# Where ScalarE casts V, and when the last two of a chunk's four result tiles are stored, in a local/global attention with a gated feed-forward layer

## The chip, the cores and the metric

The kernel runs on one core of a Trainium2 chip. A core has TensorE for matrix products (PE in the profile, its weight loads PEld), VectorE (DVE), ScalarE (ACT), GpSimd (POOL), and SyncE (SP), which here issues every DMA. Each of them works through its own list of instructions in order, and an instruction that has to wait holds up all that stand behind it in its list. The metric is device time in microseconds (us).

## The reference

There are 8 batches of 8 heads, 512 local positions and 32 global ones per head, and a head dimension of 64. A local query sees the local keys within 32 positions and all global keys; a global query sees everything. The result, 4,608 tokens of 512 values, goes through a gated layer with 1,536 hidden units. All is float32.

```
s_ll = where(|i - j| <= 32, scale * q_l @ k_l.T, -1e9)
a_l  = softmax(concat([scale * q_l @ k_g.T, s_ll]))
out_l = a_l @ concat([v_g, v_l])
out_g = softmax(scale * q_g @ k_all.T) @ v_all
x = concat([out_g, out_l])            # heads side by side: 4608 x 512
y = (sigmoid(x @ w_gate) * (x @ w_val)) @ w_out
```

## The kernel before

The tokens are cut into chunks: two halves of batch 0 (256 tokens each, interleaved), then batches 1 to 7 (512 tokens each), and at the end the 256 global tokens of all batches. While TensorE runs the feed-forward layer of one chunk (`ffn_stream`), the attention of the next is mixed into it head by head (`att_events`): a generator yields after every few products, and a queue of events with due times puts the attention's steps in between.

**The feed-forward layer.** A chunk is twelve items, one for each 128 hidden units. An item has 12 products for the gate (`bank_g`), 12 for the value (`bank_v`), both at line 389, and 12 that multiply the item before by `w_out` and add into up to four PSUM tiles (`bank_o`, line 424). Values are split into a rounded part and a rest, which is why each product is made three times. Between them ScalarE takes the tangent of the gate (L397), its absolute value (L404) and an exponential (L403), VectorE clips the gate (L402, `mn`) and multiplies (L407, L408), and `hh` is the item's result in two parts (ScalarE L410, VectorE L411).

**The result tiles.** When the last product of a chunk's twelfth item has been issued, the loop at L428 halves each `bank_o` tile into `ob`, the even ones on VectorE (L432) and the odd ones on ScalarE (L430), and SP stores it (L433, 256 KB). `ob` has two buffers, so that the third tile can be written only after the first one's transfer has landed, and the fourth after the second's.

**The attention of a head.** K and Q (`qk_raw`) and V (`v_raw`, one buffer, 256 KB, L193) are loaded. ScalarE rounds V into the left half of `vhl` (L214), and GpSimd subtracts to get the rest into the right half (L215); only then may the next head's V be loaded. `vhl` has five buffers: four heads' V are read together once more by the global queries (`global_group`, L360). Scores come from TensorE into `bank_x` (L238), VectorE adds the mask and takes the minimum (L252), ScalarE takes the exponential (L255), VectorE scales by the sum (L222), TensorE transposes (L270), ScalarE and VectorE split the result into `pt` (L281, L282), and TensorE multiplies it by `vhl` (L300, L301). Global scores go to `bank_x` and `bank_y` (L317, L319).

**Shared PSUM.** `bank_g`, `bank_v`, `bank_x` and `bank_y` share one ring of four PSUM banks, taken in turn. A product that starts a new bank waits until the bank's readers from four turns ago are done; for a bank that held a gate these are L397 and L402.

**The order.** The Python code gives the program, but a list scheduler that estimates durations decides at build time in which order each engine gets its instructions. `tc.issue_after(ins)` ties the instructions traced under it on `ins`'s engine to come behind `ins` in that engine's list; it adds no wait. The code before uses it only for the first weight conversions.

Of the kernel before, what the change touches and what calls it, by code (L numbers as in the profile page):

```python
# [8 lines left out]
F32 = mybir.dt.float32  # L9
F32R = mybir.dt.float32r  # L10
U32 = mybir.dt.uint32
AF = mybir.ActivationFunctionType
ALU = mybir.AluOpType
# [4 lines left out]
P = 128  # L18
D = 64
# [13 lines left out]
DM = 512  # L33
# [26 lines left out]
def kernel(ctx, tc, qk, v, w_gate, w_val, w_out, out_l, out_g):  # L60
    nc = tc.nc
# [10 lines left out]
    ffn = ctx.enter_context(tc.tile_pool(name="ffn", bufs=1))  # L72
# [38 lines left out]

    fill(FILL[0])
    conv_bufs = []
    anchor = [None]

    w_src = []
    for f in range(NF):
# [91 lines left out]
    def split_v(T):  # L209
        if T["native"]:  # L210
            return
        t = T["v_raw"]
        vhl = spl.tile([P, 8, 2 * D], F32R, name="vhl", bufs=GH + 1)
        nc.scalar.copy(vhl[:, :, 0:D], t)  # L214
        nc.gpsimd.tensor_tensor(vhl[:, :, D:2 * D], t, vhl[:, :, 0:D].bitcast(F32), op=ALU.subtract)  # L215
        T["v"] = vhl

# [10 lines left out]
    def local_unit(T, blocks, x32s, h, col0):  # L228
# [12 lines left out]
        if T["first"]:  # L241
            s_sb = ffn.tile([P, 2, WIN], F32, name="s_first", tag="ob", bufs=2)
# [7 lines left out]
        for i, j in enumerate(blocks):  # L250
            w = slice(*span(j))
            anchor[0] = nc.vector.tensor_tensor_reduce(  # L252
                out=s_sb[:, i, w], in0=s_ps[:, i, w], in1=mid[:, w], scale=-0.125, scalar=3.0e38,
                op0=ALU.add, op1=ALU.min, accum_out=nm[:, i:i + 1])
            nc.scalar.activation(s_sb[:, i, w], s_sb[:, i, w], AF.Exp, bias=nm[:, i:i + 1], scale=-1.0,  # L255
                                 accum_out=sm[:, i:i + 1])
        yield
        nc.vector.tensor_scalar_add(r, sm, 1e-9)
        nc.vector.reciprocal(r, r)
# [109 lines left out]
    def x_split(xt, x32, kt, x0, ntok):  # L369
        xs = slice(x0, x0 + ntok)  # L370
        nc.scalar.copy(xt[:, 0, kt, xs], x32[:, 0:ntok])
        nc.gpsimd.tensor_tensor(xt[:, 1, kt, xs], x32[:, 0:ntok], xt[:, 0, kt, xs].bitcast(F32), op=ALU.subtract)  # L372

    def ffn_stream(items):


        prev = None
        wo = None
        for n_it in range(len(items) + 1):
            if n_it < len(items):  # L380
                C, f = items[n_it]
                ntok, x0, xt = C["ntok"], C["x0"], C["xt"]()
                fs = slice(f * P, (f + 1) * P)
                for w, nm in ((wg, "bank_g"), (wv, "bank_v")):
                    acc = ps.tile([P, 512], F32, name=nm, tag="att", bufs=4)[:, 0:ntok]
                    n = 0
                    for a, c in ((0, 0), (1, 0), (0, 1)):
                        for t in range(KT):
                            nc.tensor.matmul(acc, w[a][:, t, fs], xt[:, c, t, x0:x0 + ntok],  # L389
                                             start=n == 0, stop=n == 11)  # L390
                            n += 1
                        if n < 12:
                            yield ntok / 512
                    if nm == "bank_g":
                        th = ffn.tile([P, 512], F32, name="th", bufs=1)[:, 0:ntok]
                        mn = ffn.tile([P, 512], F32, name="mn", bufs=1)[:, 0:ntok]
                        nc.scalar.activation(th, acc, AF.Tanh, scale=0.5)  # L397
                        if n_it < 2 * NF and n_it % 2:
                            nc.scalar.activation(mn, acc, AF.Relu, scale=-1.0)
                            nc.scalar.activation(mn, mn, AF.Exp, scale=-1.0)  # L400
                        else:
                            nc.vector.tensor_scalar(mn, acc, 0.0, None, op0=ALU.min)  # L402
                            nc.scalar.activation(mn, mn, AF.Exp)  # L403
                        nc.scalar.activation(th, th, AF.Abs)  # L404
                    else:

                        nc.vector.tensor_tensor(acc, acc, mn, op=ALU.mult)  # L407
                        nc.vector.scalar_tensor_tensor(acc, th, 1.0, acc, op0=ALU.add, op1=ALU.mult)  # L408
                        hh = ffn.tile([P, 2, 512], F32R, name="hh", bufs=2)
                        nc.scalar.copy(hh[:, 0, 0:ntok], acc)  # L410
                        nc.vector.tensor_tensor(hh[:, 1, 0:ntok], acc, hh[:, 0, 0:ntok].bitcast(F32), op=ALU.subtract)  # L411
                    yield ntok / 512
                if not (wo is not None and items[n_it - 1][1] == f):
                    wo = ffn.tile([P, 2, DM], F32R, name="wo", bufs=2)
                    nc.sync.dma_start(wo.bitcast(F32), wo_dram[f])
            if prev is not None:
# [5 lines left out]
                for i, (a, c) in enumerate(((0, 0), (1, 0), (0, 1))):  # L422
# [2 lines left out]
                                         start=f2 == 0 and i == 0, stop=f2 == NF - 1 and i == 2)  # L425
                    if f2 == NF - 1 and i == 2:
                        for t in range(nt):
                            ob = ffn.tile([P, DM], F32, name="ob", bufs=2)  # L428
                            if t % 2:
                                nc.scalar.mul(ob, o_ps[t], 0.5)  # L430
                            else:
                                nc.vector.tensor_scalar(ob, o_ps[t], 0.5, None, op0=ALU.mult)  # L432
                            nc.sync.dma_start(C2["dst"][t * P:(t + 1) * P, :], ob)  # L433
                    yield nt / 4
            prev = (C, f, hh, wo) if n_it < len(items) else None

# [169 lines left out]
```

## Time and profile before

| | |
|---|---|
| median of three runs | 1263.77 us (1258.55 to 1264.96) |
| the profiled execution | 1260.87 us, span 1259.1 us |
| mean granted TensorE clock | 0.975 of full speed |
| PE busy | 1182.2 us, 94% of the span |
| DVE, ACT, POOL busy | 782.3, 754.8, 414.9 us |
| SP stores of result tiles | 34, 256 KB each, 3.2 us to landing (median) |
| loads of `v_raw` | 52, 256 KB each, 2.7 us to landing (median) |

The last line of work is the feed-forward layer's, on PE, so the question for each other engine is where PE stood still for it. In rows of the profile, the number in brackets is the engine's idle time before the instruction, with what ended it. In the table of stretches the columns are the stretch, its length, the busy time (and instruction count) of PE, PEld, DVE, ACT and POOL, the granted TensorE clock as a share of full speed, the DMA engines' busy share, and GB/s. Rows with an engine name ending in q show the engine's queue of DMA issues or its sequencer.

### The profile page before, as it was taken

The numbers are of one execution on the slowest core, as the hardware profiler recorded it, in microseconds if no ns is written. First come the engines' busy times: TensorE is split into PE (matmuls) and PEld (weight loads), VectorE is DVE, ScalarE is ACT, GpSimd is POOL, SyncE is SP. The second block draws the span as 40 slices with busy tenths as digits, with TensorE's granted clock in tenths as the row PEclk, the third lists the DMA queues.
The fourth block names the chain that finished last, engine by engine and source line by source line (L and its number), as shares of the span: only waits on it lengthen the run. The fifth ranks groups of instructions, "written<-read, shape, count | busy, mean of one in ns | idle before, by whom it ended". The sixth has DMA issues, their size and how long they took to land.

```text
span 1259.1 us, 19319 instructions
## 1 busy us (share of the span) xinstructions
PE 1182.2 (94%) x6652; PEld 986.0 (78%) x6652; DVE 782.3 (62%) x2186; ACT 754.8 (60%) x1719; POOL 414.9 (33%) x408
## 2 busy tenths in 40 slices
PE   8898999999998999989998998989999899999998
PEld 6676779878786888868786887868777787888897
DVE  6789866666664676556664675656665676633343
ACT  5676776666665666646665665656665666532333
POOL 2334344423533344423533334433433334100000
PEclk9799999999999999989999998999999899999999
DMA  8678754333434333333434333343332432121243
GB/s 278 225 241 256 247 159 133 85 128 91 125 92 120 92 84 116 100 113 92 109 94 127 98 84 100 100 125 83 113 99 85 129 92 87 51 84 67 67 135 117
DMA packets 59490, 151.82 MB, mean 121 GB/s; under 512 B 6144, under 2 KB 19456, under 8 KB 59392
## 3 DMA queue, kind: packets, MB, share of 16 engines
q1 hardware_dynamic: 59392, 150.59, 39.6%
q8 instruction: 52, 0.85, 0.3%
q14 instruction: 46, 0.38, 0.1%
HBM read 135.36 MB, written 15.20 MB: 120 GB/s over the span
## 4 chain that ended last, share of the span: by engine, by line
PE 66%; DVE 11%; ACT 8%; DMA 7%; POOL 4%; issue 4%; SPq 0%; POOLq 0%; DVEq 0%; ACTq 0%
PE bank_o L424 18%; PE bank_v L389 17%; PE bank_g L389 16%; DMA v_raw<-in_v_dram 5%; PE bank_x L238 4%; PE bank_y L270 3%; POOL vhl L215 3%; ACT s_sb L255 3%; DMA out_dram<-ob 2%; DVE p_buf L222 2%; PE bank_x L300 2%; PE bank_x L301 2%; PE bank_x L317 1%; DVE xt L144 1%; DVE s_sb L252 1%
## 5 line engine op out<-in xcount | busy, mean ns | idle before, releaser
L389 PE MATMUL bank_v<-xt,wv 128*128 128x512 f32 (+1 forms) x1440 | 332.5, 368 | 9.7 <-DVE pt L282 9.7
L424 PE MATMUL bank_o<-wo,hh 128*128 128x512 f32 x1224 | 337.6, 408 | 3.0 <-DVE hh L411 2.0
L389 PE MATMUL bank_g<-xt,wg 128*128 128x512 f32 (+1 forms) x1440 | 333.8, 367 | 0.9 <-POOL xt L372 0.5
L389 PEld LDWEIGHTS bank_v<-xt,wv 128*128 128x128 f32 x1440 | 240.6, 192 | 46.6 <-issue 9.3
L389 PEld LDWEIGHTS bank_g<-xt,wg 128*128 128x128 f32 x1440 | 239.1, 191 | 38.7 <-issue 2.1
L424 PEld LDWEIGHTS bank_o<-wo,hh 128*128 128x128 f32 x1224 | 222.6, 194 | 44.5 <-DVE hh L411 2.8
L203 POOL TENSOR_TENSOR kl<-qk_raw,qk_hi 128x704 fp32r<-128x704 f32 x52 | 88.7, 1705 | 235.7 <-ACT qk_hi L202 229.2
L255 ACT ACTIVATE s_sb<-s_sb,nm 128x192 f32<-128x192 f32 (+1 forms) x240 | 110.6, 462 | 91.8 <-DVE nm L252 91.5
L305 POOL TENSOR_TENSOR x<-t 64x256 f32<-64x256 f32 x104 | 76.2, 733 | 207.5 <-DVE t L304 187.9
L222 DVE TENSOR_SCALAR p_buf<-s_sb,r 128x128 f32<-128x128 f32 (+2 forms) x443 | 116.7, 301 | 8.0 <-PE bank_y L270 2.4
L402 DVE TENSOR_SCALAR mn<-bank_g 128x512 f32<-128x512 f32 (+1 forms) x108 | 67.5, 625 | 84.1 <-ACT th L397 83.2
L411 DVE TENSOR_TENSOR hh<-bank_v,hh 128x512 fp32r<-128x512 f32 (+1 forms) x120 | 72.9, 608 | 60.7 <-ACT hh L410 60.7
L407 DVE TENSOR_TENSOR bank_v<-bank_v,mn 128x512 f32<-128x512 f32 (+1 forms) x120 | 73.7, 614 | 56.0 <-PE bank_v L389 39.8
L304 DVE TENSOR_TENSOR t<-bank_x,t 64x512 f32<-64x512 f32 x104 | 70.7, 680 | 60.5 <-ACT t L303 59.8
L397 ACT ACTIVATE th<-bank_g 128x512 f32<-128x512 f32 (+1 forms) x120 | 63.8, 531 | 73.3 <-PE bank_g L389 72.9
L410 ACT CAST hh<-bank_v 128x512 fp32r<-128x512 f32 (+1 forms) x120 | 62.6, 522 | 72.3 <-DVE bank_v L408 70.7
L252 DVE CUSTOM_DVE_ANT_0 s_sb<-bank_x,masks 128x192 f32<-128x192 f32 (+1 forms) x240 | 80.6, 369 | 34.4 <-PE bank_x L238 25.8
L215 POOL TENSOR_TENSOR vhl<-v_raw,vhl 128x512 fp32r<-128x512 f32 x52 | 67.3, 1294 | 104.0 <-ACT vhl L214 103.3
L282 DVE TENSOR_TENSOR pt<-bank_y,pt 128x512 fp32r<-128x512 f32 x104 | 71.1, 684 | 33.8 <-ACT pt L281 33.7
L270 PE MATMUL bank_y<-ident,p_buf 128*128 128x128 f32 x496 | 80.4, 282 | 10.5 <-DVE p_buf L222 5.8
L270 PEld LDWEIGHTS bank_y<-ident,p_buf 128*128 128x128 f32 x496 | 62.5, 144 | 28.8 <-DVE p_buf L222 6.7
L214 ACT CAST vhl<-v_raw 128x512 fp32r<-128x512 f32 x52 | 32.1, 618 | 87.1 <-DMA v_raw<-in_v_dram 84.8
(110 smaller groups left out, 1770.1 us busy)
## 6 DMA issues: line engine op xcount, KB each, us to landing
wo<-wo_dram SPq DMA_DIRECT2D x116, 512.0 KB, 3.6
qk_raw<-in_qk_dram SPq DMA_DIRECT2D x104, 312.0 KB, 4.5
v_raw<-in_v_dram SPq DMA_DIRECT2D x52, 256.0 KB, 2.7
out_dram<-ob SPq DMA_DIRECT2D x34, 256.0 KB, 3.2
xt<-in_w_gate_dram SPq DMA_DIRECT2D x12, 512.0 KB, 4.4
xt<-in_w_val_dram SPq DMA_DIRECT2D x12, 512.0 KB, 4.1
xt<-in_w_out_dram SPq DMA_DIRECT2D x12, 512.0 KB, 4.2
v_nat<-in_v_dram SPq DMA_DIRECT2D x8, 512.0 KB, 4.9
```

What stands on the lines that cost most here:

```text
L203: nc.gpsimd.tensor_tensor(kl, t[:, K0:Q1], hi[:, K0:Q1].bitcast(F32), op=ALU.subtract)
L215: nc.gpsimd.tensor_tensor(vhl[:, :, D:2 * D], t, vhl[:, :, 0:D].bitcast(F32), op=ALU.subtract)
L222: nc.vector.tensor_scalar(out, in_, by, None, op0=ALU.mult)
L252: anchor[0] = nc.vector.tensor_tensor_reduce(out=s_sb[:, i, w], in0=s_ps[:, i, w], in1=mid[:, w], scale=-0.125, scalar=3.0e38, op0=ALU.add ...
L255: nc.scalar.activation(s_sb[:, i, w], s_sb[:, i, w], AF.Exp, bias=nm[:, i:i + 1], scale=-1.0, accum_out=sm[:, i:i + 1])
L270: nc.tensor.transpose(pt_ps[:, 2 * i + t], pb[:, i, t * P:(t + 1) * P], ident)
L282: nc.vector.tensor_tensor(pt[:, 1], pt_ps, pt[:, 0].bitcast(F32), op=ALU.subtract)
L305: nc.gpsimd.tensor_tensor(dst, t0[:, :, 0], t0[:, :, 1], op=ALU.add)
L389: nc.tensor.matmul(acc, w[a][:, t, fs], xt[:, c, t, x0:x0 + ntok], start=n == 0, stop=n == 11)
L407: nc.vector.tensor_tensor(acc, acc, mn, op=ALU.mult)
L411: nc.vector.tensor_tensor(hh[:, 1, 0:ntok], acc, hh[:, 0, 0:ntok].bitcast(F32), op=ALU.subtract)
L424: nc.tensor.matmul(o_ps[t], ph[:, a, t * P:(t + 1) * P], pwo[:, c], start=f2 == 0 and i == 0, stop=f2 == NF - 1 and i == 2)
```

## The change

Two things are changed. The cast of V (L214) is tied behind the exponential that was traced last before it. And of a chunk's four result tiles, the last two are no longer stored where the chunk ends: they are kept in a list, and stored in the next item, after the absolute value of its gate's tangent; the odd one, on ScalarE, is tied behind that instruction. Chunks of 256 tokens have two tiles only, so for these and for the last item of all nothing is put off.

```diff
-    anchor = [None]
+    anchor, exp_at = [None], [None]
...
-        nc.scalar.copy(vhl[:, :, 0:D], t)
+        with tc.issue_after(exp_at[0].ins):
+            nc.scalar.copy(vhl[:, :, 0:D], t)
...
-            nc.scalar.activation(s_sb[:, i, w], s_sb[:, i, w], AF.Exp, bias=nm[:, i:i + 1], scale=-1.0,
-                                 accum_out=sm[:, i:i + 1])
+            exp_at[0] = nc.scalar.activation(s_sb[:, i, w], s_sb[:, i, w], AF.Exp, bias=nm[:, i:i + 1], scale=-1.0,
+                                             accum_out=sm[:, i:i + 1])
...
+    def store_out(C, t, after=None):
+        ob = ffn.tile([P, DM], F32, name="ob", bufs=2)
+        if t % 2:
+            with tc.issue_after(after.ins) if after is not None else nullcontext():
+                nc.scalar.mul(ob, C["o"][t], 0.5)
+        else:
+            nc.vector.tensor_scalar(ob, C["o"][t], 0.5, None, op0=ALU.mult)
+        nc.sync.dma_start(C["dst"][t * P:(t + 1) * P, :], ob)
...
-                        nc.scalar.activation(th, th, AF.Abs)
+                        last_th = nc.scalar.activation(th, th, AF.Abs)
+                        while later:
+                            store_out(*later.pop(0), after=last_th)
...
                         for t in range(nt):
-                            ob = ffn.tile([P, DM], F32, name="ob", bufs=2)
-                            if t % 2:
-                                nc.scalar.mul(ob, o_ps[t], 0.5)
+                            if t >= 2 and n_it < len(items):
+                                later.append((C2, t))
                             else:
-                                nc.vector.tensor_scalar(ob, o_ps[t], 0.5, None, op0=ALU.mult)
-                            nc.sync.dma_start(C2["dst"][t * P:(t + 1) * P, :], ob)
+                                store_out(C2, t)
```

The scheduler's lists show what this moves. Line numbers in the changed kernel are higher: L215 is its cast of V, L256 the exponential, L379 and L381 the tiles' halving on ScalarE and VectorE, L382 their store, L408 and L415 the tangent and the absolute value, L413 `mn`, L414 its exponential, L423 the cast of `hh`, L428 the load of `wo`.

ScalarE where a chunk ends (the tiles `bank_o_4633` and `bank_o_4635` are the second and fourth of the chunk whose stores stand at 545 us in the profile), before:

```order
L214 CAST vhl<-v_raw 128x8x64
L410 CAST hh<-bank_v 128x512
L255 ACTIVATE s_sb,sm<-s_sb,nm 128x192
L255 ACTIVATE s_sb,sm<-s_sb,nm 128x224
L214 CAST vhl<-v_raw 128x8x64
L430 ACTIVATE ob<-bank_o_4633 128x512
L255 ACTIVATE s_sb,sm<-s_sb,nm 128x224
L255 ACTIVATE s_sb,sm<-s_sb,nm 128x192
L430 ACTIVATE ob<-bank_o_4635 128x512
L397 ACTIVATE th<-bank_g 128x512
L404 ACTIVATE th<-th 128x512
```

and in the changed kernel:

```order
L423 CAST hh<-bank_v 128x512
L256 ACTIVATE s_sb,sm<-s_sb,nm 128x192
L256 ACTIVATE s_sb,sm<-s_sb,nm 128x224
L379 ACTIVATE ob<-bank_o_4633 128x512
L256 ACTIVATE s_sb,sm<-s_sb,nm 128x224
L256 ACTIVATE s_sb,sm<-s_sb,nm 128x192
L215 CAST vhl<-v_raw 128x8x64
L408 ACTIVATE th<-bank_g 128x512
L415 ACTIVATE th<-th 128x512
L379 ACTIVATE ob<-bank_o_4635 128x512
L414 ACTIVATE mn<-mn 128x512
```

The casts ahead of `hh` and between the exponentials are gone (they stand one head at a time further on), one cast stands behind the exponentials, and the fourth tile comes after the tangent and its absolute value instead of ahead of them.

SP at the same chunk end, before:

```order
L415 DMA wo<-wo_dram_112 128x1024
L193 DMA v_raw<-in_v_dram 128x512 x4
L433 DMA out_dram<-ob 128x512 x2
L415 DMA wo<-wo_dram_113 128x1024
L433 DMA out_dram<-ob 128x512 x2
```

and in the changed kernel:

```order
L428 DMA wo<-wo_dram_112 128x1024
L428 DMA wo<-wo_dram_113 128x1024
L382 DMA out_dram<-ob 128x512 x3
L193 DMA v_raw<-in_v_dram 128x512
L382 DMA out_dram<-ob 128x512
```

Four loads of V stood ahead of the first two stores, and now none does; the load of `wo` stands ahead of them instead.

ScalarE in the middle of a chunk (around 610 us in the profile), before:

```order
L214 CAST vhl<-v_raw 128x8x64
L410 CAST hh<-bank_v 128x512
L363 COPY yq<-bank_x 32x512
L214 CAST vhl<-v_raw 128x8x64
L281 CAST pt<-bank_y 128x512
L321 COPY pg_buf<-bank_x 32x512
L322 COPY pg_buf<-bank_y 32x32
L202 CAST qk_hi<-qk_raw 128x1248
L303 COPY t_6845<-bank_x 64x512
L214 CAST vhl<-v_raw 128x8x64
L281 CAST pt<-bank_y 128x512
```

and in the changed kernel:

```order
L215 CAST vhl<-v_raw 128x8x64
L423 CAST hh<-bank_v 128x512
L364 COPY yq<-bank_x 32x512
L282 CAST pt<-bank_y 128x512
L322 COPY pg_buf<-bank_x 32x512
L323 COPY pg_buf<-bank_y 32x32
L202 CAST qk_hi<-qk_raw 128x1248
L304 COPY t_6845<-bank_x 64x512
L282 CAST pt<-bank_y 128x512
```

The second and the third cast no longer stand ahead of a cast of `pt`. TensorE's list is the same in both kernels from the first full chunk on.

More of the change, by code (lines that the diff above doesn't have):

```diff
@@ L372, in x_split @@
         nc.gpsimd.tensor_tensor(xt[:, 1, kt, xs], x32[:, 0:ntok], xt[:, 0, kt, xs].bitcast(F32), op=ALU.subtract)
+    def store_out(C, t, after=None):
[6 more added lines that the diff above has]
+        nc.sync.dma_start(C["dst"][t * P:(t + 1) * P, :], ob)
     def ffn_stream(items):
         prev = None
+        later = []
         wo = None
```

## The prediction

> **What bounds the kernel now.** I read the page's totals first, then PE's waits, then the busy time by stretch, and last the chain of waits inside one of the holes.
>
> ```profile
> span 1259.1 us, 19319 instructions
> PE 1182.2 (94%) x6652; PEld 986.0 (78%) x6652; DVE 782.3 (62%) x2186; ACT 754.8 (60%) x1719; POOL 414.9 (33%) x408
> PE bank_y L319 <- DMA out_dram<-ob: 22.9, 4, 6.2
> PE bank_v L389 <- DVE pt L282: 9.7, 12, 2.7
> ACT vhl L214 <- DMA v_raw<-in_v_dram: 84.8, 36, 4.1
> L255 ACT ACTIVATE s_sb<-s_sb,nm 128x192 f32<-128x192 f32 (+1 forms) x240 | 110.6, 462 | 91.8 <-DVE nm L252 91.5
> ```
>
> PE is the bound, so its 77 us of idle time are the stake. The longest waits end with a store of a result tile (the columns are us, times, longest). The next entry ends with VectorE's half of `pt`, which waits for ScalarE's; and ScalarE itself stands 84.8 us before casts of V. (The last row gives an exponential's mean, 462 ns, used below.) Where these holes are, the stretches show. Five chunk ends, 25 us each:
>
> ```profile
> 400.00:425.00 25.00, 18.96 (x95) 15.57 (x94) 13.70 (x42) 14.19 (x32) 5.97 (x6) 0.86 0.39 121
> 542.00:567.00 25.00, 18.79 (x90) 15.31 (x91) 13.73 (x43) 13.70 (x31) 5.96 (x6) 0.86 0.39 120
> 684.00:709.00 25.00, 19.46 (x90) 16.08 (x89) 13.05 (x42) 13.70 (x31) 5.94 (x6) 0.86 0.40 121
> 830.00:855.00 25.00, 19.41 (x100) 16.02 (x99) 14.32 (x45) 13.78 (x32) 5.97 (x6) 0.93 0.42 123
> 971.00:996.00 25.00, 19.47 (x92) 16.03 (x91) 13.23 (x43) 13.70 (x31) 5.95 (x6) 0.86 0.40 122
> ```
>
> PE idles 125 less 96.1 = 28.9 us in them. The clock column shows a second loss: after each hole the granted clock is at half for some us. PE's busy time multiplied by one less the clock gives 2.7 + 2.6 + 2.7 + 1.4 + 2.7 = 12.1 us. Together **41 us**. Six stretches in mid-chunk, where the bursts of V casts lie:
>
> ```profile
> 325.00:355.00 30.00, 26.98 (x146) 22.33 (x145) 17.41 (x51) 18.78 (x39) 14.78 (x15) 1.00 0.32 95
> 467.00:487.00 20.00, 18.35 (x91) 14.98 (x89) 10.62 (x32) 11.67 (x25) 9.88 (x10) 0.91 0.40 113
> 610.00:640.00 30.00, 27.07 (x145) 22.14 (x144) 17.45 (x50) 18.54 (x40) 14.56 (x15) 1.00 0.32 95
> 750.00:790.00 40.00, 35.90 (x190) 29.44 (x190) 21.44 (x68) 23.17 (x52) 17.06 (x17) 0.91 0.35 99
> 895.00:925.00 30.00, 26.89 (x160) 22.42 (x159) 17.16 (x51) 18.94 (x40) 14.52 (x15) 1.00 0.30 94
> 1037.00:1067.00 30.00, 27.72 (x164) 23.09 (x163) 17.98 (x53) 19.21 (x41) 13.82 (x14) 1.00 0.23 75
> ```
>
> Here it is 180 less 162.9 = 17.1 us idle, and 1.7 + 3.2 = 4.9 us of clock: **22 us**. Between the holes PE has no slack:
>
> ```profile
> 640.00:680.00 40.00, 40.00 (x224) 33.70 (x223) 25.08 (x69) 25.08 (x51) 15.29 (x15) 1.00 0.40 112
> ```
>
> So ScalarE and VectorE, 63% busy there, can feed a PE that never stops; the holes are matters of order. Before 160 us PE idles another 21 us; the change hardly touches that.
>
> ```profile
> 0.00:160.00 160.00, 139.00 (x855) 107.46 (x856) 132.15 (x350) 106.09 (x293) 57.18 (x54) 0.94 0.78 250
> ```
>
> **One chunk end, step by step**, in the chain of waits and the timelines at 545 us:
>
> ```profile
> 543.20 1.31 POOL vhl L215
> 544.94 3.10 DMA out_dram<-ob
> 537.90 0.62 ACT L214 CAST vhl<-v_raw 128x512 fp32r<-128x512 f32 x1 [2.82 <-DMA v_raw<-in_v_dram]
> 542.50 0.62 ACT L214 CAST vhl<-v_raw 128x512 fp32r<-128x512 f32 x1 [2.59 <-DMA v_raw<-in_v_dram]
> 529.91 14.94 SPq L193 DMA_DIRECT2D v_raw<-in_v_dram  x4
> 535.85 0.70 DVE L408 SCALAR_TENSOR_TENSOR bank_v<-th,bank_v 128x512 f32<-128x512 f32 x1
> 540.55 0.68 DVE L432 TENSOR_SCALAR ob<-bank_o 128x512 f32<-128x512 f32 x1
> 542.27 0.35 DVE L252 CUSTOM_DVE_ANT_0 s_sb<-bank_x,masks 128x192 f32<-128x192 f32 x1
> 548.07 0.69 DVE L432 TENSOR_SCALAR ob<-bank_o 128x512 f32<-128x512 f32 x1 [5.43 <-DMA out_dram<-ob]
> 549.98 0.69 DVE L402 TENSOR_SCALAR mn<-bank_g 128x512 f32<-128x512 f32 x1 [0.94 <-ACT th L397]
> 544.23 0.28 PE L317 MATMUL bank_x<-kl,qk_hi 128*32 128x256 f32 x1
> 550.72 0.24 PE L319 MATMUL bank_y<-qk_hi 128*32 128x32 f32 x1 [6.21 <-DMA out_dram<-ob]
> ```
>
> A V is loaded, cast, reduced by GpSimd, and only then the next is loaded, 4.6 us from cast to cast. ScalarE has four of these casts early in its list and waits for each load. SP has the four loads ahead of the first two stores, so the first tile, ready at 541.2, leaves at 544.94. The third tile waits for its landing until 548.07; the tangent stands behind the fourth on ScalarE, `mn` behind the tangent, and the PSUM bank that PE wants at 544.5 is free only when `mn` is done at 550.7. Both parts of the change strike at this chain.
>
> **The change part by part.** No instruction is added: 52 casts (0.62 us each), their GpSimd subtractions and loads, and 34 tiles and stores stay, only in other places.
>
> *The cast of V.* A load now goes out one head ahead and its cast stands behind an exponential, with 17 or more ScalarE instructions between it and the `pt` cast of its head from the first full chunk on (counted in the new list). The wait of 84.8 us should go, and GpSimd's subtraction, 1.3 us, is done long before PE asks for it. In mid-chunk this frees the `pt` cast:
>
> ```profile
> 613.27 0.62 ACT L214 CAST vhl<-v_raw 128x512 fp32r<-128x512 f32 x1 [2.34 <-DMA v_raw<-in_v_dram]
> 615.28 0.39 PE L300 MATMUL bank_x<-pt,vhl 128*128 128x256 f32 x1 [1.25 <-DVE pt L282]
> ```
>
> ScalarE gains 2.34 us there, PE lost 1.25, so the hole closes. Of the 22 us I leave 0.5 for each of the six places: **gain 19 us**; the ends are 0 and 22.
>
> *The chunk end.* `hh` can be cast when L408 is done, at 536.6 and not at 538.4, and with it the exponentials, the sums and the first tile come 1.6 us earlier: ready at 539.6. Nothing blocks SP, whose load of `wo` ahead of the store waits for the products that the tile waits for too. With the 3.1 us of the row above the store lands at 542.8. Meanwhile VectorE does the rest up to the third tile; its masks, now done at 542.6, end at 541.0, two exponentials later it is about 542.1, and it would get there at 542.5. The tile runs from 542.8 to 543.5. On ScalarE a V cast (0.62 us, to 542.7) and the tangent, of like size, to 543.3, come first, so `mn` runs to 544.2, just before PE wants the bank at 544.5: no stall. The dearest store in the chain bounds it from above:
>
> ```profile
> 1109.13 5.19 DMA out_dram<-ob
> ```
>
> Landing after 5.2 us, the third tile ends at 545.6, `mn` at 546.3, and PE stands 1.8 us. Behind the tangent ScalarE has the absolute value, the fourth tile, the exponential of `mn` and the cast of `pt`, then comes VectorE's half: five of about 0.62 us, so `pt` is ready near 546.4, where PE, after four L424 products, asks at about 545.5: 0.9 us. So a chunk end keeps between 0.9 and 2.7 us; I take 1.5, nearer the ordinary landing. The fourth tile's bank is asked for only when the first three of these products are out, at about 545.2, and is free by 544.5; hidden.
>
> The clock after so short a hole: two rows differ.
>
> ```profile
> 473.00:476.00 3.00, 3.00 (x13) 2.50 (x13) 0.68 (x1) 1.79 (x3) 2.65 (x3) 0.56 0.77 249
> 918.30:921.00 2.70, 2.70 (x15) 2.30 (x16) 0.80 (x2) 1.87 (x5) 0.00 (x0) 1.00 0.05 18
> 472.73 0.39 PE L300 MATMUL bank_x<-pt,vhl 128*128 128x256 f32 x1 [1.65 <-DVE pt L282]
> 918.28 1.17 PE L389 MATMUL bank_v<-xt,wv 128*128 128x512 f32 x4 [1.73 <-DVE pt L282]
> ```
>
> After 1.65 us the clock fell to half, with 1.65 us lost in its stretch; after 1.73 us it stayed. I take half of that, 0.8 us a chunk end. The Trainium skill ("TensorE: Matmul & The Clock Gate", "Why this matters for your kernels") says that only idle gaps above about 3 us drop the clock; by it this term is zero and the sum 4 us lower. The first of the two rows speaks against it.
>
> A chunk end thus keeps 2.3 us, five keep 11.5, and of the 41 us **29.5 are gained**, with ends of 15 and 41. The two-tile stores and the weight conversions' changed order in the first 265 us I put at nothing, give or take 4.
>
> *Sum.* 1260.87 - 29.5 - 19 = 1212.4; with the runs before spread over 1258.55 to 1264.96 and a median 2.9 above the profiled one, I say **1213 us**.
>
> **The rivals.**
>
> *The store's landing still ends the wait* (20%). For it: `ob` keeps two buffers, `mn` still stands behind the third tile, and 512 KB of `wo` go out right ahead of the first store. Against it: at 545 us 3.7 us of the wait were SP's loads and not the landing. Each end would keep 2.7 us and the clock's 2.4: 26 in all, a gain of 15, plus 19: 1227 us.
>
> *All of it goes* (12%). For it: the 40 us without a hole. Against: the 0.9 us of `pt`. 41 and 22 us: 1198 us.
>
> *The waits only move* (5%). PE's holes come back in other places as soon as VectorE and ScalarE, each at 63%, meet a PE that never waits; 1255 to 1267 us.
>
> *Slower: V's casts hold up the next head's keys* (4%). In the new lists the cast stands ahead of the tangent or of a `pt` cast, and its subtraction ahead of `kl` on GpSimd. If every head's tangent and keys came late by 0.62 and 1.29 us and PE felt all of it, 52 heads would cost 99 us against the 48.5 gained: 1311 us. It decides from 0.93 us a head. Against it: GpSimd is the one that waits.
>
> ```profile
> POOL kl L203 <- ACT qk_hi L202: 229.2, 38, 10.1
> ACT th L397 <- PE bank_g L389: 72.9, 61, 3.8
> ```
>
> Both the keys' subtraction and the tangent mostly wait for others, so there is room ahead of them.
>
> **How the numbers follow.** The forecast has 59%, the rivals 20, 12, 5 and 4. The range reaches from the second rival less its 3 or so of spread to the first with the worst mid-chunk (gain 8 less): 1195 to 1236 us. Outside lie the last two rivals and the edges. What this measurement can tell from no change is about 0.5%, 6 us. Faster by more: 59 + 20 + 12 = 91%; within: 5%; slower: 4%.
>
> **What would show it.** The row of L319 with the store as its releaser should fall from 22.9 us to a few, and the 84.8 us of ScalarE for V to nearly none; 25 us around a chunk end should read above 23 us busy with a clock of 0.95 or more, and SP's timeline shows no run of four V loads. PE's busy total falls too, by some 13 us (12.1 and 4.9, less five times 0.8), since its slow phases end. I am wrong if the chunk ends still have holes of 3 us or more: then the landing, not the order, was the bound. If the ends are clean but the time is above 1240, the next line of waits is in the attention itself, at `pt` or `p_buf`.

## The result, and the profile after

The changed kernel takes 1200.47 us (median of four runs, 1199.79 to 1203.23) against 1263.56 us for the kernel before (four runs, 1258.55 to 1264.96): a ratio of 0.951, 95% interval 0.948 to 0.954, so 5% faster. The prediction was 1213 us with a range of 1195 to 1236. The time lies in the range, but nearer to the rival "all of it goes" (1198 us) than to the forecast, and it got there in another way than either said.

The head of the page, the shares of the chain that ended last, and the first of PE's own waits, after the change:

```profile
span 1197.8 us, 19349 instructions
PE 1160.7 (97%) x6652; PEld 973.6 (81%) x6652; DVE 807.5 (67%) x2186; ACT 753.0 (63%) x1719; POOL 417.3 (35%) x408
PE 72%; DVE 10%; ACT 5%; issue 2%; POOL 1%; DMA 0%; DVEq 0%; ACTq 0%; POOLq 0%
PE bank_v L400 <- DVE pt L283: 11.8, 12, 1.0
```

Before, DMA held 7% of that chain and ScalarE 8%; now they hold 0% and 5%. ScalarE's 84.8 us of waits for V are gone from the table of waits, and so is PE's wait of 22.9 us for a store. One row is left at the top: twelve waits of 1.0 us at most for VectorE's half of `pt`. Before, the same row held 9.7 us in twelve waits of up to 2.7 us.

**Where the time came from.** A pair of stretches with the same work, from just behind the small chunks' stores to just behind those of the last full chunk (the same two products of PE's list), first before and then after (stretch, length, busy time of PE, PEld, DVE, ACT and POOL, the clock, the DMA share, GB/s):

```profile
270.96:1110.55 839.59, 792.33 (x4290) 662.15 (x4289) 526.68 (x1523) 521.68 (x1129) 312.99 (x313) 0.98 0.34 99
```

```profile
262.96:1051.11 788.15, 776.22 (x4289) 651.92 (x4288) 551.24 (x1523) 521.37 (x1131) 318.87 (x316) 1.00 0.37 107
```

The stretch is 51.4 us shorter: PE's idle time in it fell from 47.3 to 11.9 us, which is 35.3, and its busy time by 16.1 us, as the clock no longer drops. VectorE is busier by 25 us for the same number of instructions; that row returns below.

The five chunk ends, in stretches of 25 us as the prediction read them:

```profile
375.00:400.00 25.00, 25.00 (x143) 21.12 (x142) 15.07 (x43) 14.29 (x34) 7.25 (x7) 1.00 0.31 99
517.00:542.00 25.00, 25.00 (x135) 20.86 (x134) 17.90 (x56) 17.78 (x41) 7.26 (x7) 1.00 0.48 146
659.00:684.00 25.00, 25.00 (x136) 21.16 (x135) 17.49 (x51) 16.42 (x34) 11.95 (x12) 1.00 0.40 116
780.00:805.00 25.00, 25.00 (x134) 20.95 (x134) 18.53 (x57) 15.73 (x38) 7.27 (x7) 1.00 0.41 122
915.00:940.00 25.00, 24.88 (x134) 20.61 (x133) 17.65 (x54) 17.46 (x40) 7.28 (x7) 1.00 0.48 146
```

Nothing is left of the holes there: 0.1 us idle in 125, at full clock. The chunk end that stood at 545 us is now 19.0 us earlier (the last product ahead of the hole starts at 525.22 and not at 544.23 us); in its timeline the stores leave SP, and the third tile, `mn` and `pt` are made, in this order:

```profile
518.67 0.33 SPq L428 DMA_DIRECT2D wo<-wo_dram  x1
519.15 0.68 DVE L381 TENSOR_SCALAR ob<-bank_o 128x512 f32<-128x512 f32 x1
519.87 4.37 SPq L382 DMA_DIRECT2D out_dram<-ob  x3
521.98 0.60 ACT L215 CAST vhl<-v_raw 128x512 fp32r<-128x512 f32 x1
522.48 0.59 ACT L408 ACTIVATE th<-bank_g 128x512 f32<-128x512 f32 x1
523.18 0.69 DVE L381 TENSOR_SCALAR ob<-bank_o 128x512 f32<-128x512 f32 x1 [0.71 <-DMA out_dram<-ob]
523.79 0.68 DVE L413 TENSOR_SCALAR mn<-bank_g 128x512 f32<-128x512 f32 x1
525.22 0.28 PE L318 MATMUL bank_x<-kl,qk_hi 128*32 128x256 f32 x1
525.34 0.18 PE L320 MATMUL bank_y<-qk_hi 128*32 128x32 f32 x1
525.64 0.69 DVE L283 TENSOR_TENSOR pt<-bank_y,pt 128x512 fp32r<-128x512 f32 x1 [0.39 <-ACT pt L282]
526.42 0.36 PE L301 MATMUL bank_x<-pt,vhl 128*128 128x256 f32 x1
```

No load of V stands ahead of the stores. The first tile leaves as soon as it is made; VectorE still waits 0.71 us for its landing, 3.3 us after the issue, but that wait is covered: `mn` is done at 524.47, and the product that needs its bank starts at 525.34 with no idle time before it. The product of `pt` follows just as closely.

**In mid-chunk** there were two kinds of holes. Those at the products of `pt` itself (L300 before; seven in these chunks, 8.5 us in all) are gone. Twelve of nearly equal length are left, two in each chunk. They stand at the same twelve products of PE's list that the row `bank_v L389 <- DVE pt` counted before: there seven of them waited 0.15 to 0.26 us and five 0.93 to 2.65, and now all wait 0.97 to 0.99. The timeline of one:

```profile
420.36 0.57 ACT L282 CAST pt<-bank_y 128x512 fp32r<-128x512 f32 x1
420.46 1.69 DVE L223 TENSOR_SCALAR p_buf<-s_sb,r 128x128 f32<-128x128 f32 x4
420.53 1.36 POOL L216 TENSOR_TENSOR vhl<-v_raw,vhl 128x512 fp32r<-128x512 f32 x1 [2.01 <-ACT vhl L215]
422.06 0.68 DVE L283 TENSOR_TENSOR pt<-bank_y,pt 128x512 fp32r<-128x512 f32 x1
422.89 1.17 PE L400 MATMUL bank_v<-xt,wv 128*128 128x512 f32 x4 [0.99 <-DVE pt L283]
```

ScalarE's half of `pt` is ready at 420.93, but VectorE has four scalings ahead of its half, and these take 1.69 us here. In the kernel before the same four stood ahead of it too, at each of the twelve places, and took 0.86 to 0.88 us. The four of one place with their product, and the product of before that matches the one at 422.89:

```profile
629.28 0.87 DVE L222 TENSOR_SCALAR p_buf<-s_sb,r 128x128 f32<-128x128 f32 x4
630.89 1.16 PE L389 MATMUL bank_v<-xt,wv 128*128 128x512 f32 x4 [1.38 <-DVE pt L282]
439.11 1.16 PE L389 MATMUL bank_v<-xt,wv 128*128 128x512 f32 x4 [0.17 <-DVE pt L282]
```

GpSimd's subtraction of V runs beside them now. Whether it is the cause is what the later experiments ask.

### The profile page after: what moved, and what is told of

Its sections match the earlier page's. It is cut to its first block, busy times and chain, and to the rows that moved or that the text cites. A ratio compares the mean times of both kernels' runs of the same rounds, so it can differ in the third digit from the quotient of the medians.

```text
span 1197.8 us, 19349 instructions
## 1 busy us (share of the span) xinstructions
PE 1160.7 (97%) x6652; PEld 973.6 (81%) x6652; DVE 807.5 (67%) x2186; ACT 753.0 (63%) x1719; POOL 417.3 (35%) x408
## 4 chain that ended last, share of the span: by engine, by line
PE 72%; DVE 10%; ACT 5%; issue 2%; POOL 1%; DMA 0%; DVEq 0%; ACTq 0%; POOLq 0%
PE bank_v L400 19%; PE bank_g L400 19%; PE bank_o L437 19%; PE bank_y L271 3%; DVE p_buf L223 3%; PE bank_x L239 3%; ACT s_sb L256 2%; PE bank_x L301 2%; PE bank_x L302 2%; PE bank_x L318 2%; PE bank_x L361 1%; DVE bank_v L420 1%; DVE pt L283 1%; DVE bank_v L421 1%; DVE mn L413 1%
## 5 line engine op out<-in xcount | busy, mean ns | idle before, releaser
L400 PE MATMUL bank_v<-xt,wv 128*128 128x512 f32 (+1 forms) x1440 | 329.3, 365 | 11.8 <-DVE pt L283 11.8
L437 PE MATMUL bank_o<-wo,hh 128*128 128x512 f32 x1224 | 329.0, 400 | 0.9 <-ACT hh L423 0.4
L400 PEld LDWEIGHTS bank_v<-xt,wv 128*128 128x128 f32 x1440 | 238.2, 190 | 49.3 <-PE bank_y L320 12.6
L437 PEld LDWEIGHTS bank_o<-wo,hh 128*128 128x128 f32 x1224 | 217.2, 189 | 40.8 <-ACT hh L423 1.4
L256 ACT ACTIVATE s_sb<-s_sb,nm 128x192 f32<-128x192 f32 (+1 forms) x240 | 110.7, 462 | 102.6 <-DVE nm L253 102.2
L223 DVE TENSOR_SCALAR p_buf<-s_sb,r 128x128 f32<-128x128 f32 (+2 forms) x443 | 145.8, 370 | 7.6 <-PE bank_y L271 1.9
L203 POOL TENSOR_TENSOR kl<-qk_raw,qk_hi 128x704 fp32r<-128x704 f32 x52 | 88.6, 1704 | 112.0 <-ACT qk_hi L202 111.5
L423 ACT CAST hh<-bank_v 128x512 fp32r<-128x512 f32 (+1 forms) x120 | 62.7, 522 | 95.9 <-DVE bank_v L421 95.1
L408 ACT ACTIVATE th<-bank_g 128x512 f32<-128x512 f32 (+1 forms) x120 | 63.7, 531 | 89.5 <-PE bank_g L400 88.9
L413 DVE TENSOR_SCALAR mn<-bank_g 128x512 f32<-128x512 f32 (+1 forms) x108 | 67.5, 625 | 73.2 <-ACT th L408 73.2
L253 DVE CUSTOM_DVE_ANT_0 s_sb<-bank_x,masks 128x192 f32<-128x192 f32 (+1 forms) x240 | 80.8, 370 | 38.7 <-PE bank_x L239 35.8
L271 PE MATMUL bank_y<-ident,p_buf 128*128 128x128 f32 x496 | 76.7, 275 | 6.6 <-DVE p_buf L223 5.6
L205 POOL TENSOR_TENSOR qk_hi<-qk_raw,qk_hi 64x256 fp32r<-64x256 f32 x104 | 80.4, 794 | 4.1
```

Source lines behind the costliest of these rows:

```text
L203: nc.gpsimd.tensor_tensor(kl, t[:, K0:Q1], hi[:, K0:Q1].bitcast(F32), op=ALU.subtract)
L205: nc.gpsimd.tensor_tensor(hi[64:128, r], t[64:128, r], hi[64:128, r].bitcast(F32), op=ALU.subtract)
L223: nc.vector.tensor_scalar(out, in_, by, None, op0=ALU.mult)
L253: anchor[0] = nc.vector.tensor_tensor_reduce(out=s_sb[:, i, w], in0=s_ps[:, i, w], in1=mid[:, w], scale=-0.125, scalar=3.0e38, op0=ALU.add ...
L256: exp_at[0] = nc.scalar.activation(s_sb[:, i, w], s_sb[:, i, w], AF.Exp, bias=nm[:, i:i + 1], scale=-1.0, accum_out=sm[:, i:i + 1])
L271: nc.tensor.transpose(pt_ps[:, 2 * i + t], pb[:, i, t * P:(t + 1) * P], ident)
```

## The experiments

The theory was that of the prediction: the casts of V, queued in fours behind their loads, hold up ScalarE, and their loads hold up SP ahead of the stores; tying the cast removes both. Rivals were that the stores' new place does the work, and that the gain comes from one of the two kinds of places only. Each ratio below is to runs of the kernel before that were taken beside it (medians of 1262.86 to 1263.86 us).

### The tie of V alone

The changed kernel with all four tiles stored where the chunk ends, as before:

```diff
-                            if t >= 2 and n_it < len(items):
+                            if False:
                                 later.append((C2, t))
```

> Only the cast of V is tied behind the exponential; all four tiles are stored where the chunk ends, as before. In the scheduler's lists every engine's rows are those of the changed kernel, row for row, so theory one (the cast's place is the whole change) expects 1200.5 us, within 4 us. Theory two (the later stores bring a part of the 63 us) would need at least 10 us more than that, 1211 or above, with a hole of 1 us or more at the chunk ends.

Measured: 1202.89 us (1199.64 to 1205.97), ratio 0.951 (0.948 to 0.954). The scheduler's lists of this kernel are the same, row for row on all five engines, as those of the changed kernel. So the two programs are one, and the second half of the change adds nothing to the first: once V is tied, the scheduler by itself puts the fourth tile behind the tangent and its absolute value.

### The stores alone

The kernel before with the new stores, and no tie (as an edit of the changed kernel):

```diff
-        with tc.issue_after(exp_at[0].ins):
-            nc.scalar.copy(vhl[:, :, 0:D], t)
+        nc.scalar.copy(vhl[:, :, 0:D], t)
```

> Only the last two tiles are stored later; the casts of V stay in their bursts, and SP still has four loads of V ahead of the first two stores. Theory one: the third tile still waits for the first store's landing, and only the tangent no longer stands behind the fourth tile, so that mn comes about 1.2 us earlier at each of five chunk ends: 1255 to 1259 us, holes at chunk ends of about 5 us. Theory two (the stores' place is worth a third of the gain or more): 1242 or less, holes of 3 us or less.

Measured: 1257.45 us (1252.99 to 1264.77), ratio 0.995 (0.993 to 0.998). PE's first wait names `mn` in place of the store, but VectorE's third tile, which stands ahead of `mn`, still waits for the first store's landing, and SP still has the four loads ahead of that store (the chunk end of 545 us):

```profile
PE bank_y L319 <- DVE mn L412: 24.7, 6, 5.2
531.22 15.30 SPq L193 DMA_DIRECT2D v_raw<-in_v_dram  x4
549.77 0.69 DVE L380 TENSOR_SCALAR ob<-bank_o 128x512 f32<-128x512 f32 x1 [5.45 <-DMA out_dram<-ob]
```

What moved is the tangent, which no longer stands behind the fourth tile and is done ahead of the third now, so that `mn` starts 0.9 us after the tile does and not 1.9: the longest hole falls from 6.2 to 5.2 us and no further. The store's landing was the last link of the chain that the profile named, but not what made it late.

### One kind of place at a time

V's cast tied only for the heads whose casts stood at the chunk ends (1 to 4), and, in a second kernel, only for the others; both leave the first three chunks untied and store as before:

```diff
-        with tc.issue_after(exp_at[0].ins):
+        with tc.issue_after(exp_at[0].ins) if T["h"] in (1, 2, 3, 4) and not T["early"] else nullcontext():
```

> The tie for the casts of heads 1 to 4 only, from the first full chunk's attention on (these are the casts of the burst at the chunk ends); stores as before. Theory one: the chunk ends lose all their 41 us of idle time and clock, the mid-chunk bursts stay with 22: about 1222 us, holes at chunk ends under 0.5 us. If the landing of the stores keeps a part of the hole (the prediction's 2.3 us each): 1233 us.

> The tie for the casts of heads 5, 6, 7 and 0 only (the bursts in mid-chunk); stores as before. Theory one: the mid-chunk holes go, but the two holes of 1 us a chunk that the changed kernel shows come in their place, so 22 less 12 us are gained: about 1253 us; the chunk ends keep 5 holes of 5.5 to 6.2 us and their slow clock. If the two bursts are one mechanism (a cast late in mid-chunk also makes the chunk end late), the ends shrink too and the time is under 1240.

Measured: 1222.76 us (1221.76 to 1225.14), ratio 0.967 (0.964 to 0.969), for the ends; 1242.88 us (1239.29 to 1245.53), ratio 0.983 (0.980 to 0.986), for mid-chunk. PE's longest waits, first of the kernel with only the ends tied:

```profile
PE bank_v L400 <- DVE pt L283: 17.0, 12, 2.7
PE bank_x L301 <- POOL vhl L216: 8.3, 6, 1.5
```

then of the one with only mid-chunk tied:

```profile
PE bank_y L320 <- DMA out_dram<-ob: 24.1, 4, 6.3
PE bank_v L400 <- DVE pt L283: 6.8, 12, 1.0
```

Each tie closes its own holes, but for waits of about 1 us, and leaves the others. In the kernel with only mid-chunk tied these waits stand at six of the twelve products, one in each chunk. The gains, 3.3% and 1.7%, add up to the 4.9% of the full tie within its interval. The ends came out where they were expected; mid-chunk, expected at 1253 us, gave 10 us more. The expectation counted 12 us for two new waits of 1 us in each chunk, and only one came (the row holds 6.8 us, where it held 9.7 before); another part may be the start of the program, which is told of below.

### A second buffer for V instead of the tie

The kernel before, with nothing tied:

```diff
-        t = raw.tile([P, 8, D], F32, name="v_raw")
+        t = raw.tile([P, 8, D], F32, name="v_raw", bufs=2)
```

(and a smaller scratch area for the DMA rings, 512 in place of 1024, to make room for it).

> The kernel before, untied, with two buffers for V's load instead of one; nothing else (the room for it is taken from an unused scratch area of the DMA's). ScalarE's list still has the casts early and in a burst of four, and SP still four loads of V ahead of the stores. If the serial chain of load, cast and subtraction through one buffer is what makes the burst dear, two heads overlap, the burst takes some 8 us instead of 15, the first store leaves about 4 us earlier and most of the slow clock goes: about 1222 us, 1210 to 1235. If only the place in the lists counts, the time stays within 8 us of 1263.

Measured: 1211.39 us (1208.31 to 1212.65), ratio 0.958 (0.955 to 0.961). SP's four loads ahead of the stores, and ScalarE's wait for V:

```profile
517.30 7.26 SPq L193 DMA_DIRECT2D v_raw<-in_v_dram  x4
```

```profile
ACT vhl L214 <- DMA v_raw<-in_v_dram: 35.8, 23, 3.2
```

The run of four loads is still there, but it holds SP for 7.26 us instead of 14.94, and ScalarE's wait falls from 84.8 to 35.8 us. Most of the gain is to be had without a tie. With the loads two at a time, four casts close together cost much less. But the scheduler's order changed with the buffer as well: at the chunk ends no cast stands between the tangent and `hh` or between the exponentials any more, and the fourth tile stands behind the tangent. The expectation had ScalarE's list unchanged; how much of the gain is the buffer's and how much the order's, this run does not part.

### VectorE's half of `pt` ahead of two scalings

For the twelve holes that the change left, the first question was whether VectorE's order makes them. The changed kernel, with the last two of each unit's four scalings tied behind VectorE's half of the `pt` traced before:

```diff
         for i, j in enumerate(blocks):
-            main = s_sb[:, i, 32:224].rearrange("p (a c) -> p a c", c=96)[:, :, 0:64]
+            with tc.issue_after(pt_at[0].ins) if i == 1 and not nat and pt_at[0] is not None else nullcontext():
+                main = s_sb[:, i, 32:224].rearrange("p (a c) -> p a c", c=96)[:, :, 0:64]
...
-            nc.vector.tensor_tensor(pt[:, 1], pt_ps, pt[:, 0].bitcast(F32), op=ALU.subtract)
+            pt_at[0] = nc.vector.tensor_tensor(pt[:, 1], pt_ps, pt[:, 0].bitcast(F32), op=ALU.subtract)
```

> The changed kernel, with the second two of a unit's four scalings (p_buf) tied behind VectorE's half of the pt before. In the changed kernel twelve holes of 0.98 us are left on PE, each ended by that half, which stands behind four scalings (1.69 us) on VectorE. If VectorE's order is the cause, they close: two scalings less ahead is 0.85 us, so the 11.8 us shrink to 1 to 3, and the time to about 1191 us. If ScalarE's half of pt (behind the cast of V) is the cause, nothing changes: 1200 us.

Measured: 1188.67 us (1185.53 to 1190.33), ratio 0.940 (0.937 to 0.942), the fastest of all. The middle of the program, first of the changed kernel and then of this one:

```profile
250.00:1000.00 750.00, 738.12 (x4081) 619.78 (x4079) 528.32 (x1473) 502.03 (x1092) 308.54 (x304) 1.00 0.38 110
```

```profile
250.00:1000.00 750.00, 749.81 (x4150) 628.84 (x4149) 517.98 (x1494) 507.81 (x1106) 313.73 (x310) 1.00 0.39 112
```

All twelve holes are closed: of 750 us PE idles 0.2. The 11.8 us of the wait and the 11.8 us between the medians agree.

### V's cast behind the cast of `pt`

The other way to bring `pt` forward is on ScalarE. V's cast tied behind ScalarE's last half of `pt` instead of the last exponential, alone and together with the edit above:

```diff
-            exp_at[0] = nc.scalar.activation(s_sb[:, i, w], s_sb[:, i, w], AF.Exp, bias=nm[:, i:i + 1], scale=-1.0,
-                                             accum_out=sm[:, i:i + 1])
+            nc.scalar.activation(s_sb[:, i, w], s_sb[:, i, w], AF.Exp, bias=nm[:, i:i + 1], scale=-1.0,
+                                 accum_out=sm[:, i:i + 1])
...
-            nc.scalar.copy(pt[:, 0], pt_ps)
+            exp_at[0] = nc.scalar.copy(pt[:, 0], pt_ps)
```

> The changed kernel, with the cast of V tied behind ScalarE's last cast of pt and not behind the last exponential: in ScalarE's list the two change places, and on VectorE one of the four scalings falls behind its half of pt in the places with a hole. If ScalarE's order is the cause of the twelve holes, all close (1189 us); if VectorE's is, each loses about a scaling, 0.25 to 0.4 us: 1196 us.

> Both of the two edits before. By VectorE's order alone: as with the scalings tied, about 1191 us. If each closes a part, 1189 us. Not below 1186, since the first 160 us keep 17 us of idle time that neither touches.

Measured: alone 1208.79 us (1204.08 to 1210.42), ratio 0.956 (0.953 to 0.959), a miss; with the other edit 1194.33 us (1192.12 to 1194.93), ratio 0.944 (0.942 to 0.947). Alone, ScalarE's half came earlier as meant, 0.6 us ahead of the first scaling and not 0.1, and the holes grew all the same, from 11.8 to 14.5 us:

```profile
424.48 0.56 ACT L282 CAST pt<-bank_y 128x512 fp32r<-128x512 f32 x1
424.95 0.62 ACT L215 CAST vhl<-v_raw 128x512 fp32r<-128x512 f32 x1
425.09 1.88 DVE L223 TENSOR_SCALAR p_buf<-s_sb,r 128x128 f32<-128x128 f32 x4
425.64 1.27 POOL L216 TENSOR_TENSOR vhl<-v_raw,vhl 128x512 fp32r<-128x512 f32 x1 [2.49 <-ACT vhl L215]
```

The expected change on VectorE did not come: at all twelve places four scalings still stand ahead of `pt`. They now take 1.88 us, and they end just after the subtraction on GpSimd does. ScalarE was not what `pt` waited for. (The rest of the loss lies elsewhere: the profile shows small waits at other products and a start 3.9 us later.)

With both edits the twelve holes are closed (of 750 us PE idles 1.7), at 3 us more than expected: five waits of 0.34 us for another tile and one of 1.4 us for a result tile are left. The scalings of this kernel are held as long as those of the changed kernel, whose row, shown below, has 145.8 us:

```profile
L223 DVE TENSOR_SCALAR p_buf<-s_sb,r 128x128 f32<-128x128 f32 (+2 forms) x443 | 146.0, 364 | 7.8 <-PE bank_y L272 1.9
```

So it is enough that `pt` comes ahead of the scaling that is held.

### Is it the subtraction on GpSimd?

Two kernels ask. In the first the subtraction is issued as two halves; the lists of all other engines stay the same:

```diff
-        nc.gpsimd.tensor_tensor(vhl[:, :, D:2 * D], t, vhl[:, :, 0:D].bitcast(F32), op=ALU.subtract)
+        [nc.gpsimd.tensor_tensor(vhl[:, q:q + 4, D:2 * D], t[:, q:q + 4], vhl[:, q:q + 4, 0:D].bitcast(F32), op=ALU.subtract) for q in (0, 4)]
```

> The changed kernel, with GpSimd's subtraction of V (128x512, 1.30 us) issued as two subtractions of 128x256; the rows of all other engines stay as they are. Theory (a VectorE scaling that meets the subtraction stands still until it ends): a half takes some 0.76 us by the row of the 64x256 subtraction, so if VectorE gets its turn between the halves the longest of the four scalings falls from 1.10 to about 0.5 to 0.6 us, the twelve holes from 0.98 to about 0.4 us, and the time to about 1194 us. If it gets no turn between them the scaling takes about 1.3 us, the holes 1.2 us, 1203 us. Rival (the scalings are long for another reason, and GpSimd only happens to run beside them): the four still take 1.69 us, the holes 0.98 us, 1200 us.

In the second it is moved to VectorE, behind its half of `pt`:

```diff
-        nc.gpsimd.tensor_tensor(vhl[:, :, D:2 * D], t, vhl[:, :, 0:D].bitcast(F32), op=ALU.subtract)
+        with tc.issue_after(pt_at[0].ins) if pt_at[0] is not None else nullcontext():
+            nc.vector.tensor_tensor(vhl[:, :, D:2 * D], t, vhl[:, :, 0:D].bitcast(F32), op=ALU.subtract)
```

> The changed kernel, with the subtraction of V moved from GpSimd to VectorE, tied behind VectorE's half of pt; the four scalings keep their place ahead of pt. Theory (the scalings stand still beside GpSimd's subtraction): with nothing on GpSimd there the four take 0.87 us as they did before the change, pt is ready 0.8 us earlier, the twelve holes shrink to about 0.2 us, and the time falls to about 1190 us although VectorE gets some 31 us more work (52 subtractions of about 0.6 us). Rival (the order of VectorE's list alone makes the holes, four scalings ahead of pt instead of three): the holes stay at about 1 us and the time at 1200 us, or above it where the added work on VectorE delays the next one.

Measured: the halves 1200.05 us (1199.13 to 1201.94), ratio 0.950 (0.948 to 0.953), no change; on VectorE 1192.04 us (1188.74 to 1197.80), ratio 0.945 (0.942 to 0.947). The four scalings of one hole taken by themselves (shortest, median and longest in ns, first and last start), in the changed kernel, with the halves, and with the subtraction on VectorE:

```profile
L223 DVE TENSOR_SCALAR p_buf<-s_sb,r x4: 243/298/1096, 420.5 to 421.9; 128x128 f32<-128x128 f32 x2, 128x96 f32<-128x96 f32 x1, 128x64 f32<-128x64 f32 x1
```

```profile
L223 DVE TENSOR_SCALAR p_buf<-s_sb,r x4: 288/424/736, 420.6 to 421.5; 128x128 f32<-128x128 f32 x2, 128x96 f32<-128x96 f32 x1, 128x64 f32<-128x64 f32 x1
```

```profile
L224 DVE TENSOR_SCALAR p_buf<-s_sb,r x4: 251/282/307, 417.8 to 418.4; 128x128 f32<-128x128 f32 x2, 128x96 f32<-128x96 f32 x1, 128x64 f32<-128x64 f32 x1
```

In the changed kernel one scaling of the four takes 1.10 us and the others their usual 0.24 to 0.31. With the subtraction off GpSimd all four are short again, `pt` comes 0.8 us sooner, and the twelve holes shrink as the theory said, to the 0.15 to 0.18 us that most of these places had before the change:

```profile
PE bank_v L402 <- DVE pt L285: 2.0, 12, 0.2
```

Four scalings still stand ahead of `pt` there, so the order of VectorE's list is not what made the holes grow. (The rival as written down had three of them ahead of `pt` before the change; the lists have four, before and after.) The kernel with only mid-chunk tied says the same within one run: at the six products where the subtraction falls beside the scalings these take 1.68 to 1.69 us and PE waits 0.97 to 0.99, at the other six 0.87 us and 0.15 to 0.18.

The halves came out in neither of the two ways written down. The longest scaling did fall, to 0.74 us, about the length of one half, so VectorE gets a turn between the halves; but the scaling after it meets the second half, and the four together take 1.62 us instead of 1.69. Cutting GpSimd's work in two gives VectorE next to nothing back: it loses 0.75 us instead of 0.82. Over the whole program the rows of the scalings, before, after, and with the subtraction on VectorE:

```profile
L222 DVE TENSOR_SCALAR p_buf<-s_sb,r 128x128 f32<-128x128 f32 (+2 forms) x443 | 116.7, 301 | 8.0 <-PE bank_y L270 2.4
```

```profile
L223 DVE TENSOR_SCALAR p_buf<-s_sb,r 128x128 f32<-128x128 f32 (+2 forms) x443 | 145.8, 370 | 7.6 <-PE bank_y L271 1.9
```

```profile
L224 DVE TENSOR_SCALAR p_buf<-s_sb,r 128x128 f32<-128x128 f32 (+2 forms) x443 | 117.2, 306 | 7.6 <-PE bank_y L273 1.9
```

The 29 us that the scalings grew by over the whole program account for the 25 us of VectorE in the stretches above, and they go with the subtraction.

## Why the prediction was right, and where its sum was not

| step | gain predicted | measured in the profiles |
|---|---|---|
| five chunk ends | 29.5 us of 41 | 41: idle 28.9 to 0.1, clock 12.1 to 0 |
| mid-chunk | 19 us of 22, in six stretches | 11.2: from 22 and 1.0 us outside these stretches to 11.8, in twelve places |
| the first 260 us | 0, give or take 4 | 8.5 in this pair of profiles |

The first two rows can be checked against SP's rows for the second pair of stores of the small chunks and the last pair of all, first before, then after:

```profile
262.90 0.81 SPq L433 DMA_DIRECT2D out_dram<-ob  x2
1254.64 0.81 SPq L433 DMA_DIRECT2D out_dram<-ob  x2
```

```profile
254.41 0.81 SPq L382 DMA_DIRECT2D out_dram<-ob  x2
1194.31 0.81 SPq L382 DMA_DIRECT2D out_dram<-ob  x2
```

The first pair comes 8.5 us sooner, the last 60.3, so 51.8 us were gained between them, against 41 + 11.2 = 52.2 by the table and 48.5 in the prediction. That the sum came within 4 us is partly luck: two terms were wrong by 11.5 and 7.8 us in opposite directions. Of the 12.5 us by which the forecast of 1213 us was too long, the larger part in this pair of profiles is the start, of which the prediction had no account.

**The mechanism held.** SP's run of four V loads, the late stores, the third tile's wait, `mn` behind it: the tie of V alone undoes all of it, and the stores alone do not. The prediction had the two parts strike at the chain together; the second one adds nothing to the first, and alone it gives about 6 us (1257.45 against 1263.86).

**The chunk end was mis-sized: 2.3 us kept, 0 measured.** The step that failed is the walk through the lists, in where it starts. The landing was put well (3.1 us, measured 3.3, and the third tile at 542.8 against 523.18 + 19.0 = 542.2). But by the walk the V cast would end at 542.7 and the tangent at 543.3; they ended at 522.58 and 523.07, which is 541.6 and 542.1 on the old scale, since VectorE's masks and the exponentials behind them were done 0.8 and 1.0 us sooner than counted. The walk took the end of L408, 536.6, from the trace of before as it stood. But there that item's tangent had stood behind a cast of V as well (the cast at 532.44, the tangent at 533.09), and with the cast gone L408's counterpart ended at 516.98, which is 536.0: 0.6 us sooner, most of the difference. So `pt`, put at 546.4 with 0.9 us of PE's time lost, was ready at 526.33, which is 545.3, and PE did not wait for it. The upper bound, a landing of 5.2 us, did not occur there. With no hole there was nothing for the clock to fall after, so the 0.8 us a chunk end that was taken for it fell away too, and the Trainium skill's 3 us ("TensorE: Matmul & The Clock Gate", "Why this matters for your kernels") was not tested at these places.

**Mid-chunk was mis-sized the other way: 3 us kept, 11.8 measured.** The step said: ScalarE gains 2.34 us, PE lost 1.25, so the hole closes. For the hole it walked, at a product of `pt` (L300), and for the six others of that kind this came true. It was then taken for all, and the other kind, the twelve waits of the row with 9.7 us, was not walked. There `pt` waits for VectorE's half, which stands behind four scalings before as after. What the prediction did not look for is that GpSimd's subtraction now falls beside these scalings and holds one of them for 0.8 us; it counted the subtraction only as being "done long before PE asks for it". The trace of before had the price to show, though not at these twelve places: one scaling, at 173.15 us, takes 1.07 us beside the subtraction of V (172.84 to 174.14), and 27 take 0.37 to 0.65 us beside GpSimd's subtraction of 64x256, where 0.28 is usual.

**The clock.** PE's busy total was to fall by 13 us, and fell by 21.5. In the stretches of the same work it is 16.1, close to the 12.1 + 4.9 that the prediction had as lost to the clock before it kept 4 of them; 4.9 lie ahead of these stretches, where the clock differs from one profile to the next (0.96 and 0.97 in this pair).

**The start stays open.** Its term was put at nothing, give or take 4, and this pair of profiles shows 8.5. But the second pair of stores stands at 257.24 us in the kernel with the same lists as the changed one, and not at 254.41. Over five profiles with the tie there it is at 253.16 to 257.34 (mean 255.4), over five without it at 257.36 to 262.90 (mean 260.0), and in the two with the cast tied behind `pt` at 257.54 and 258.33. A few microseconds of gain are likely, the size is not settled.

**The rivals.** That the store's landing still ends the wait is out: the landing takes its 3.3 us and PE does not feel it. That everything goes is right for the chunk ends and wrong for mid-chunk. That the waits only move holds in small: the twelve waits of the row with 9.7 us hold 11.8 us now, eight of them longer than before and four shorter. That V's casts would hold up the next head's keys did not happen; GpSimd's wait for their cast fell from 229.2 us, but 111.5 are left, and PE's waits name neither the keys' subtraction nor the tangent.

## What to carry to other kernels

When a wait ends with a transfer, look at what stood ahead of its issue: here a queue of loads that each wait for a buffer made the store late. A tie that spreads the loads cured it; a second buffer, with the order that the scheduler then chose, cured most of it; moving the store did not. After a move, follow the awaited tile on every engine that makes a part of it, and ask what will now run beside it, since an instruction's own length can change with its neighbour on another engine. The holes that remain after a success are worth a look of their own: one more tie, VectorE's half of `pt` ahead of two scalings, closed all twelve.

## What the runs showed of the hardware

One of VectorE's scalings from SBUF to SBUF stands still while GpSimd's subtraction runs: 1.10 us instead of 0.29, and the four together 1.69 instead of 0.87; with the subtraction off GpSimd they take 0.87 again. Not every VectorE instruction does. The scalings of 128x96 are not held: in the changed kernel 24 of them begin inside the subtraction and take 0.30 to 0.31 us, as they do alone; those that are held are of 128x128 and 128x64. In the fastest kernel VectorE's half of `pt`, which reads one operand from PSUM, runs wholly beside the subtraction and keeps its length, and of the scalings behind it one is held:

```profile
421.17 1.36 POOL L216 TENSOR_TENSOR vhl<-v_raw,vhl 128x512 fp32r<-128x512 f32 x1 [2.01 <-ACT vhl L215]
421.61 0.69 DVE L284 TENSOR_TENSOR pt<-bank_y,pt 128x512 fp32r<-128x512 f32 x1
422.21 0.56 DVE L223 TENSOR_SCALAR p_buf<-s_sb,r 128x128 f32<-128x128 f32 x2
```

The Trainium skill ("SBUF — State Buffer", "Who interferes with whom") states this as a lock: the two engines share a pair of ports to SBUF, an instruction that takes it keeps it to its end, the other engine stands still meanwhile, and VectorE's instructions with at most one SBUF input outside certain fast modes do not need it. The rows above agree on each point that they touch. In this kernel the scaling behind `pt` is held for 0.1 us only, since less of the subtraction is left by then; in the one with both edits it is held for 0.6 to 0.7 us, and the twelve holes are closed there too.
